# A fused attention and gated-MLP kernel: the planner's prices for VectorE and ScalarE changed, and the order of TensorE's work searched again

## The chip, the cores and the metric

One core of a Trainium2 chip runs the whole program. The metric is the device time of one execution in microseconds (us). The kernel before takes 1592.65 us, the median of three runs (1592.35 to 1593.04).

## What is computed

With x of 2048 tokens by 512 features, 32 query heads of 16 features and one shared key and value head:

```python
q = (x @ wq).reshape(B, S, H, Dh).transpose(0, 2, 1, 3)
k, v = x @ wk, x @ wv
p = softmax(einsum("bhqd,bkd->bhqk", q, k) * Dh ** -0.5)
a = einsum("bhqk,bkd->bhqd", p, v).transpose(0, 2, 1, 3).reshape(B, S, H * Dh) @ wo
b = (sigmoid(x @ w_gate) * (x @ w_up)) @ w_down
g = sigmoid((x * gate_w).sum(-1, keepdims=True))
out = g * a + (1 - g) * b
```

## The kernel before, in words

Everything passes through TensorE and the eight banks of PSUM, each 128 partitions by 512 words of fp32. Attention is cut into 32 units, each of four heads by 512 tokens, and each unit into 16 chunks of 128 keys. A unit needs three kinds of matmul. **Maxima** (function `maximum`, L1126 and L1128): scores with tokens on partitions, of which VectorE takes each row's maximum (TENSOR_REDUCE, 2048 of them in all). **Scores** (`scores`, L1135 and L1137): the same scores with keys on partitions and the maximum already subtracted through an extra row of the contraction, of which ScalarE takes the exponential into a tile p (2048). **Values** (`pv`, L1010): the four p tiles of a chunk against v, as four matmuls side by side in 32 columns each, summed in one bank, which is later copied out into a tile ou (`sums_out`, L1018) by ScalarE or VectorE; where a unit's sum is copied out more than once, GpSimd adds the copies (`sum_add`, L1021). Beside attention stand the **fills** (`fill`, L1105), 4404 matmuls of the MLP and of the output projection, whose results leave their bank in a gate (ScalarE), a product (VectorE) or a scaled copy (`part_of`, L1084 on VectorE or L1086 on ScalarE), or are added onto a tile by VectorE (`add`, L1065). At the start stand the projections of x to keys, values and queries (L864).

Maxima, scores and fills each use 64 rows of the array, so two of them run at once, one in the upper half (h = 0) and one in the lower (h = 1). Such a pair is called a step here. Values use all 128 rows in strips of 32 columns. TensorE goes back and forth between the two shapes: some steps, then a run of values chunks, and so on.

The order of all this is one string, ORDER (L670), found by a search outside the kernel. Each character is a step: a hexadecimal digit packs what the two halves do (0 nothing, 1 a maximum, 2 a score, 3 a fill), `V` is a values chunk, `G` a projection, `T` the turning of a unit's maxima, `C` copies the running sum out so that another bank can take the sums, `.` lets the plan's clock pass 25 units. `plan()` replays the string in a class State, which keeps a clock in its own units and decides by it, while it replays, which bank a matmul takes, which engine makes a copy (`evacuate`), and between which instructions of the other queues loads, stores and GpSimd's tasks go. The instructions are then issued in that order on every engine. At run time nothing of the plan's clock is left: each instruction waits on semaphores for what it needs, and no longer.

State prices work as follows (units of its clock):

```python
self.now += 100                                                   # a step
self.now += VALUES                                                # a chunk of values
if self.full: self.now += OUT                                     # from values to steps
if not self.full: self.now += IN                                  # from steps to values
self.free[i] = self.on("dve", self.now + LATE, RED) + TAIL + FREE # a maximum's bank
at = self.on("act", self.now + LATE_A, EXP) + TAIL_A              # an exponential
self.free[i] = at + FREE_A
```

So a bank read by VectorE counts as free TAIL + FREE units after VectorE's instruction is priced to end, one read by ScalarE TAIL_A + FREE_A units after its own; and a step may only take a bank that the plan has as free. SUM is the price of VectorE's addition, SCALED that of ScalarE's scaled copy (VectorE's is SCALED_D), LATE_V the time from the last values chunk to the copy of its sum.

Of the kernel before, what the change touches and what calls it, by code (L numbers as in the profile page):

```python
# [53 lines left out]
IN, OUT, VALUES, TURN = 52, 94, 371, 20  # L54
# [15 lines left out]
LATE_V = 130  # L70
# [46 lines left out]
class State:  # L117
# [558 lines left out]
    "f6fedf5dVVVVC67b7bbfdb7bedff7fede7e7efbfededfbdef6ff57VVVVV6edef76fbf6efddebf7b7b7b7bfb7afdb7fefededddVVVC6f6def"
    "edb7b7efbdb7f6fdVV999VVC7e7bf6f6fedb7bedbfdfdTVVVC6deeeddfef6f9ff9dbf6fee7b7fbdef9dbff7bb7777V99aV666V699V659VV6"
    "eddbfb7b7ddVVC6b7bfdbd7ddeVVC6deedfbdbbdfbddbfbededfb76fefedbdbfe77777VVV67baV95aV9a5V6TaV696VC6f9bfdbdfd7aVVC9d"
    "eedfeb77b7VVded9bffb79f6fbdefe7b7e7b7ef7ef6f9feb7ffde5dVVC655VVVC6b6ffdedeb7b7fefdefTbfb7bf7b9fededfe7efeb57VV6a"
    "5V999V699V996V65aV65aV999V656VV9deeddbfde7efeeffb7b7bfbfb7b7e7bfbdffdd5dVVVC69edffedeedfe7f77b7efedebffb7bfdbfbd"  # L680
    "f7757VVVVVC9b77bfe7bdbe7fe7f9fe7beddbfeeTffe7bf7fdedd5VVVVC97bfb7edef9f6f9fedfedef6fbd9fb7ef6f9fff5777VVVV6f6fbd"
    "9fbf6b7f9ffed6fef9fb7edef75VVC9e9ff76fff5aVVVVCdadff67bfb7bdbedfedb7ef6f7eb7ef7edbf9ff6f5dVVVaaTVVVC9bdfb7bdbf9f"
    "b77bedfedef9fe7edbbdfedb76fff6dV9a9V696V669V969V666VC699V669VC669V66aV6a5V996V95aV966VCdeTeeff7bf9b7f9f6fed77VVC"
    "9b77bf9fef9dbf7efed7ddVVVV9e9ffdedef9fbdb7ffde7bfeedefde7ff7b7b7777VVVVC97bfbdb7b7efe76fe7fedbf9def6faf7def9fedf"
    "f75VVVC7bTbfef9ff9b7fbd9fedddVVVC6b7fe7b7b7bfe7bffb7be7e7e7fefb67VVVC9f9fedb7bf9ef7e7fe7fdddddVVV9e6f7fede7eeVVV"
# [12 lines left out]
    "ef6bdfbdbdbf7e7bff7775VVVVV6b97ffed7be7bff9fed7fbebff7e7fedeedb7f7ddVVVVC97bfededbb7bf7eeddfbededfe7be7f9fedbfe7"
# [540 lines left out]
```

## Time and profile before

| | |
|---|---|
| median of three runs | 1592.65 us |
| the profiled execution's own time | 1592.79 us |
| its span, first to last instruction | 1591.0 us |
[...]
| VectorE busy | 1406.1 us (88%) |
| ScalarE busy | 1194.6 us (75%) |
| GpSimd busy | 909.2 us (57%) |

The profiled execution lies 0.14 us over the median and 1.8 us over its own span. The busy time of TensorE is that of pipelined matmuls whose ends are modelled, so 99% says that some matmul was always under way, not that none came late. How fast TensorE really goes is read from when its instructions start, in the chain of waits and the timeline.

### The profile page before, as it was taken

The page shows a single profiled execution, that of the slowest core. Times are in us where ns is not written, and L with a number is a line of the kernel's source. Part 1 is how long each engine was busy: PE and PEld are TensorE (multiplying, and loading weights), DVE is VectorE, ACT ScalarE, POOL GpSimd, SP SyncE. Part 2 cuts the span into 40 slices and gives each one's busy share as a digit, 9 for nine tenths or more (in the row PEclk, how much of TensorE's full clock was granted, in tenths as well). Part 3 has the DMA queues.
Part 4 walks back from the last instruction along what each step waited for, and adds up shares of the span by engine and source line. Part 5 has one row for each costly group of instructions (what it writes and reads, how often), then busy time and mean ns, then how long its engine had stood idle before and what let it go on. Part 6 is the DMA issues. An engine that isn't in the chain of part 4 may idle for free.

```text
span 1591.0 us, 33696 instructions
## 1 busy us (share of the span) xinstructions
PE 1582.7 (99%) x12950; PEld 1008.2 (63%) x12950; DVE 1406.1 (88%) x2443; ACT 1194.6 (75%) x2358; POOL 909.2 (57%) x705
## 2 busy tenths in 40 slices
PE   9999999999999999999999999999999999999998
PEld 7776666566665666565664766666566566666644
DVE  6899989999889988999899989999989989899952
ACT  5266778787788777778778776787877877777797
POOL 4348554737664564674673656565766365568332
PEclk9999999999999999999999999999999999999999
DMA  7412111215121211114121121111512021111011
GB/s 229 149 51 71 54 40 38 59 31 137 35 75 31 76 59 45 42 55 104 55 72 32 59 68 42 49 58 32 137 29 81 24 83 59 45 42 31 9 36 44
DMA packets 52230, 98.12 MB, mean 62 GB/s; under 512 B 17960, under 2 KB 19240, under 8 KB 51044
## 3 DMA queue, kind: packets, MB, share of 16 engines
q1 hardware_dynamic: 52068, 95.96, 20.4%
q8 instruction: 101, 1.65, 0.4%
q14 instruction: 61, 0.50, 0.1%
HBM read 74.05 MB, written 8.90 MB: 52 GB/s over the span
## 4 chain that ended last, share of the span: by engine, by line
PE 99%; DVE 0%; DMA 0%; ACT 0%; SPq 0%; issue 0%; DVEq 0%; ACTq 0%
PE bank L1105 32%; PE bank L1010 30%; PE bank L1135 17%; PE bank L1126 16%; PE bank L864 3%; DMA xf<-x_in 0%; DVE mx L1128 0%; PE bank L995 0%; PE bank L1178 0%; ACT x L782 0%; PE bank L934 0%; SPq L767 0%; DVE ba L1187 0%; DVEq L1235 0%; ACT q L956 0%
## 5 line engine op out<-in xcount | busy, mean ns | idle before, releaser
L1128 DVE TENSOR_REDUCE mx<-bank 128x1 f32<-128x512 f32 x2048 | 1258.7, 680 | 121.9 <-PE bank L1126 80.7
L1137 ACT ACTIVATE p<-bank 128x512 f32<-128x512 f32 x2048 | 1038.1, 657 | 46.4 <-PE bank L1135 27.6
L1135 PE MATMUL bank<-qs,ks 64*128 64x512 f32 x2048 | 730.9, 405 | 0.0
L1126 PE MATMUL bank<-ks,qs 62*128 62x512 f32 x2048 | 694.4, 406 | 0.0
L1010 PE MATMUL bank<-p,v_aug 128*32 128x512 f32 x4096 | 487.2, 598 | 0.0
L1135 PEld LDWEIGHTS bank<-qs,ks 64*128 64x128 f32 x2048 | 354.2, 185 | 132.0 <-issue 32.7
L1126 PEld LDWEIGHTS bank<-ks,qs 62*128 62x128 f32 x2048 | 346.4, 185 | 121.8 <-DVE mx L1128 40.9
L1018 ACT COPY ou<-bank 128x512 f32<-128x512 f32 x135 | 79.5, 589 | 291.8 <-PE bank L1010 213.1
L1105 PE MATMUL bank<-wd,hl 64*128 64x512 f32 x1344 | 271.6, 391 | 0.0
L1010 PEld LDWEIGHTS bank<-p,v_aug 128*32 128x32 f32 x4096 | 109.6, 109 | 244.1 <-issue 212.6
L1021 POOL TENSOR_TENSOR ou<-ou,ou 128x512 f32<-128x512 f32 x106 | 137.1, 1293 | 138.1 <-ACT ou L1018 135.1
L1105 PEld LDWEIGHTS bank<-wd,hl 64*128 64x128 f32 x1344 | 201.6, 185 | 15.6
L1105 PE MATMUL bank<-x,wu 64*128 64x512 f32 x672 | 185.8, 392 | 0.0
L1105 PE MATMUL bank<-xs,wg 64*128 64x512 f32 x672 | 185.1, 392 | 0.0
L1105 PE MATMUL bank<-x,wg 64*128 64x512 f32 x672 | 183.9, 391 | 0.0
L1105 PE MATMUL bank<-xs,wu 64*128 64x512 f32 x672 | 182.6, 392 | 0.0
L982 POOL TENSOR_TENSOR qs<-stage,qs 16x1024 fp32r<-16x1024 f32 x62 | 148.6, 2396 | 4.8
L1105 PEld LDWEIGHTS bank<-x,wg 64*128 64x128 f32 x672 | 111.8, 185 | 9.3 <-issue 2.0
L1105 PEld LDWEIGHTS bank<-x,wu 64*128 64x128 f32 x672 | 112.6, 185 | 7.6 <-POOL wg L839 0.8
L1105 PEld LDWEIGHTS bank<-xs,wu 64*128 64x128 f32 x672 | 111.6, 185 | 5.8
L1105 PEld LDWEIGHTS bank<-xs,wg 64*128 64x128 f32 x672 | 111.1, 185 | 6.1
L1089 POOL TENSOR_TENSOR ba<-ba,pa_d 128x512 f32<-128x512 f32 x48 | 61.9, 1289 | 89.9 <-DVE ba L1065 77.6
(92 smaller groups left out, 1129.7 us busy)
## 6 DMA issues: line engine op xcount, KB each, us to landing
rg<-wg SPq DMA_DIRECT2D x28, 512.0 KB
ru<-wu SPq DMA_DIRECT2D x28, 512.0 KB
rd<-wd SPq DMA_DIRECT2D x28, 512.0 KB
stage<-qd SPq DMA_DIRECT2D x192, 64.0 KB
xs<-x SPq DMA_DIRECT2D x16, 512.0 KB
xf<-x_in SPq DMA_DIRECT2D x16, 256.0 KB
qd<-q SPq DMA_DIRECT2D x16, 256.0 KB
ra<-wo SPq DMA_DIRECT2D x8, 512.0 KB
```

Of the source, the lines that this page charges most:

```text
L864: nc.tensor.matmul(ps, w[:, p, part(kc)], X[b, kc][:, q, :], start=i == 0, stop=i == 3 * KC - 1)
L982: e.tensor_tensor(qs[r], stage[r], f32(qs[r]), op=ALU.subtract)
L1010: nc.tensor.matmul(ps[32 * j:32 * j + 32, :], v_aug[:, c, :], PT.pop((u, c, j)), start=new, stop=last)
L1018: (nc.scalar.copy if e == "act" else nc.vector.tensor_copy)(OU[i], ps)
L1021: nc.gpsimd.tensor_tensor(OU[n], OU[n], OU[i], op=ALU.add)
L1089: nc.gpsimd.tensor_tensor(BA[b, t], BA[b, t], PA.pop((b, t)), op=ALU.add)
L1105: nc.tensor.matmul(banks[i], l, r, start=at == 0, stop=at == j.n - 1)
L1126: nc.tensor.matmul(banks[i], qs_t[u % 3][r, pr, part(qt)], ks[r, kb * 512:(kb + 1) * 512], start=True, stop=True)
L1128: nc.vector.tensor_reduce(MX[u][:, pr, h, qt, kb:kb + 1], banks[i], axis=AX.X, op=ALU.max)
L1135: nc.tensor.matmul(banks[i], ks[r, part(c)], qs_t[u % 3][r, pr, :], start=True, stop=True)
L1137: nc.scalar.activation(p, banks[i], AF.Exp, scale=0.25)
```

## The change

Five lines of prices and one string. No function, tile, buffer or instruction kind changes.

```diff
-LATE, LATE_A, FREE, FREE_A = 190, 200, 65, 60
+LATE, LATE_A, FREE, FREE_A = 190, 200, 48, 62
-RED, GATED, SUM, ENDS, PARTS, INVERSE = 260, 258, 285, 60, 325, 70
-EXP, COPY, SCALED = 208, 210, 247
+RED, GATED, SUM, ENDS, PARTS, INVERSE = 257, 258, 288, 60, 325, 70
+EXP, COPY, SCALED = 209, 210, 258
-IN, OUT, VALUES, TURN = 52, 94, 371, 20
+IN, OUT, VALUES, TURN = 52, 94, 369, 20
-LATE_V = 130
+LATE_V = 120
 ORDER = (
-    "GGGGGGGG555G555G555G555GG555GG555GGG555GG555G555G555Gdd55GTfffdf777ff7f777ffffffefb7edbf7b7f9fb7efdef79ffedbe7de"
+    "GGGGGGGG555G555G555G555GGG555G555GG555GGG555G555G555G555GT7ffff7fdffdf7fff7f77fee7ef76fef7ffde7ef97bbfdbdf9fbbdd"
...
```

The rest of ORDER is another string of the same kind. Counted in the two strings, and in the instructions that come of them:

| | before | after |
|---|---|---|
| values chunks | 512 | 512 |
| runs of values chunks (of one chunk; of five) | 230 (93; 11) | 222 (88; 21) |
| runs of projections | 12 | 12 |
| steps (with one half empty) | 4256 (12) | 4257 (14) |
| `.` | 2 | 10 |
| `C` | 106 | 101 |
| copies of a sum, L1018: ScalarE; VectorE | 135; 2 | 129; 3 |
| scaled copies: ScalarE, L1086; VectorE, L1084 | 59; 21 | 49; 31 |
| GpSimd's additions of sums, L1021 | 106 | 101 |

Every other kind of instruction keeps its count on every engine, and so do the transfers on SP's queue.

On TensorE, in unit 3, before: chunks 10 and 11 of the values (the second number in the name of p) stand alone between three steps each.

```order
L1010 MATMUL bank2_74<-p3_10_0_0_3301,v_aug_105 32x512
L1010 MATMUL bank2_74<-p3_10_0_1_3196,v_aug_105 32x512
L1010 MATMUL bank2_74<-p3_10_1_0_3292,v_aug_105 32x512
L1010 MATMUL bank2_74<-p3_10_1_1_3178,v_aug_105 32x512
L1135 MATMUL bank5_77<-qs0_132,ks_128 128x512
L1126 MATMUL bank1_73<-ks_128,qs2_134 128x512
L1135 MATMUL bank6_78<-qs0_132,ks_128 128x512
L1126 MATMUL bank0_72<-ks_128,qs2_134 128x512
L1135 MATMUL bank7_79<-qs0_132,ks_128 128x512
L1135 MATMUL bank3_75<-qs1_133,ks_128 128x512
L1010 MATMUL bank2_74<-p3_11_0_0_3333,v_aug_105 32x512
L1010 MATMUL bank2_74<-p3_11_0_1_3258,v_aug_105 32x512
```
The same unit on TensorE in the change: chunks 9, 10 and 11 follow each other.

```order
L1126 MATMUL bank4_76<-ks_128,qs2_134 128x512
L1010 MATMUL bank3_75<-p3_9_0_0_3119,v_aug_105 32x512
L1010 MATMUL bank3_75<-p3_9_0_1_3230,v_aug_105 32x512
L1010 MATMUL bank3_75<-p3_9_1_0_3101,v_aug_105 32x512
L1010 MATMUL bank3_75<-p3_9_1_1_3191,v_aug_105 32x512
L1010 MATMUL bank3_75<-p3_10_0_0_3156,v_aug_105 32x512
L1010 MATMUL bank3_75<-p3_10_0_1_3238,v_aug_105 32x512
L1010 MATMUL bank3_75<-p3_10_1_0_3126,v_aug_105 32x512
L1010 MATMUL bank3_75<-p3_10_1_1_3234,v_aug_105 32x512
L1010 MATMUL bank3_75<-p3_11_0_0_3197,v_aug_105 32x512
```
What moved: the steps that stood between the chunks now stand before and after the run (unit 3 goes from nine runs of values to six, other units go from fewer to more).

On VectorE, in unit 19's maxima before: the second token tile of block 2 (ba2_1) gets its first part from ScalarE, and VectorE only adds onto it.

```order
L1128 TENSOR_REDUCE mx19_11198<-bank2_74 128x1
L1128 TENSOR_REDUCE mx19_11198<-bank3_75 128x1
L1128 TENSOR_REDUCE mx19_11198<-bank0_72 128x1
L1065 SCALAR_TENSOR_TENSOR ba2_1_11730<-bank1_73,gom_131,ba2_1_11730 128x512
L1128 TENSOR_REDUCE mx19_11198<-bank4_76 128x1
L1128 TENSOR_REDUCE mx19_11198<-bank2_74 128x1
L1128 TENSOR_REDUCE mx19_11198<-bank6_78 128x1
```
The same place on VectorE in the change (the name before the arrow is the tile written):

```order
L1128 TENSOR_REDUCE mx19_11269<-bank5_77 128x1
L1128 TENSOR_REDUCE mx19_11269<-bank4_76 128x1
L1084 TENSOR_SCALAR ba2_1_11676<-bank6_78,gom_131 128x512
L1128 TENSOR_REDUCE mx19_11269<-bank7_79 128x1
L1128 TENSOR_REDUCE mx19_11269<-bank4_76 128x1
L1128 TENSOR_REDUCE mx19_11269<-bank5_77 128x1
L1128 TENSOR_REDUCE mx19_11269<-bank3_75 128x1
L1065 SCALAR_TENSOR_TENSOR ba2_1_11676<-bank0_72,gom_131,ba2_1_11676 128x512
```
What moved: the scaled copy into ba2_1 is now VectorE's, between two maxima, where the maxima behind it come one instruction later.

## Rows read from the trace of the kernel before

**Rows 1.** The page: span, busy time by engine, chain that ended last.

```profile
span 1591.0 us, 33696 instructions
PE 1582.7 (99%) x12950; PEld 1008.2 (63%) x12950; DVE 1406.1 (88%) x2443; ACT 1194.6 (75%) x2358; POOL 909.2 (57%) x705
...
PE 99%; DVE 0%; DMA 0%; ACT 0%; SPq 0%; issue 0%; DVEq 0%; ACTq 0%
PE bank L1105 32%; PE bank L1010 30%; PE bank L1135 17%; PE bank L1126 16%; PE bank L864 3%; DMA xf<-x_in 0%; DVE mx L1128 0%; PE bank L995 0%; PE bank L1178 0%; ACT x L782 0%; PE bank L934 0%; SPq L767 0%; DVE ba L1187 0%; DVEq L1235 0%; ACT q L956 0%
```
**Rows 2.** The two longest waits of TensorE's matmuls, whole span (us, times, longest).

```profile
PE bank L886 <- POOL v_aug L880: 1.3, 1, 1.3
PE bank L1164 <- ACT ou_last L1162: 0.5, 1, 0.5
```
**Rows 3.** The chain in time (start us, us, what), values runs around 210 us.

```profile
205.94 4.43 PE bank L1010 x40
210.37 0.43 PE bank L1126
...
220.64 3.57 PE bank L1010 x32
```
**Rows 4.** Groups of TensorE's matmuls between those two runs, 210.3 to 220.55 us.

```profile
L1105 PE MATMUL bank<-xs,wg 64*128 64x512 f32 x24 | 7.1, 396 | 0.0
L1135 PE MATMUL bank<-qs,ks 64*128 64x512 f32 x19 | 7.0, 395 | 0.0
L1105 PE MATMUL bank<-x,wg 64*128 64x512 f32 x24 | 6.9, 392 | 0.0
L1126 PE MATMUL bank<-ks,qs 62*128 62x512 f32 x19 | 6.6, 400 | 0.0
```
**Rows 5.** The chain in time, values runs of one chunk, 471 to 488 us.

```profile
471.06 0.99 PE bank L1010 x8
...
472.94 1.00 PE bank L1010 x8
...
488.10 1.00 PE bank L1010 x8
```
**Rows 6.** Timeline of VectorE and ScalarE (start us, us) near 401 and 211 us.

```profile
401.12 5.47 DVE L1128 TENSOR_REDUCE mx<-bank 128x1 f32<-128x512 f32 x9 [1.74 <-PE bank L1126]
401.18 5.02 ACT L1137 ACTIVATE p<-bank 128x512 f32<-128x512 f32 x10
...
210.83 11.64 DVE L1128 TENSOR_REDUCE mx<-bank 128x1 f32<-128x512 f32 x19 [1.71 <-PE bank L1126]
```
**Rows 7.** Who waited for the maxima on VectorE, whole span (us, times).

```profile
  PEld bank L1126: 40.9, 51
  PEld bank L1135: 32.2, 39
  PEld bank L1010: 11.6, 35
  PEld bank L995: 3.5, 6
```
**Rows 8.** Groups on VectorE, ScalarE and GpSimd, whole span (count, busy us, mean ns, idle).

```profile
L1128 DVE TENSOR_REDUCE mx<-bank 128x1 f32<-128x512 f32 x2048 | 1258.7, 680 | 121.9 <-PE bank L1126 80.7 <-PE bank L1135 33.4 <-PE bank L1105 4.2
L1084 DVE TENSOR_SCALAR pa_d<-bank,gom 128x512 f32<-128x512 f32 x13 | 9.6, 741 | 0.0
L1018 ACT COPY ou<-bank 128x512 f32<-128x512 f32 x135 | 79.5, 589 | 291.8 <-PE bank L1010 213.1 <-issue 37.4 <-POOL ba L1089 8.2
L1086 ACT ACTIVATE pa_d<-bank,gom 128x512 f32<-128x512 f32 x35 | 25.9, 741 | 0.0
L1021 POOL TENSOR_TENSOR ou<-ou,ou 128x512 f32<-128x512 f32 x106 | 137.1, 1293 | 138.1 <-ACT ou L1018 135.1 <-DVE ou L1018 2.4
```
**Rows 9.** The chain by line in shares of the span, and its longest VectorE piece.

```profile
by line: PE bank L1105 32.5%; PE bank L1010 29.6%; PE bank L1135 16.7%; PE bank L1126 16.1%; PE bank L864 3.3%; DMA xf<-x_in 0.3%; DVE mx L1128 0.2%; PE bank L995 0.2%; PE bank L1178 0.1%; ACT x L782 0.1%; PE bank L934 0.1%; issue 0.1%; SPq
...
61.30 3.59 DVE mx L1128 x6
```

More of the change, by code (lines that the diff above doesn't have):

```diff
@@ L676 @@
[L676 to L685, printed above, removed]
@@ new lines @@
+    "efe7bd9ffedbdb7fddf5VVVVVC99ffb7bdbf9f6fede7fbdee77eefdedbf9fdff77577VVVVC67bb7b7fbb7edfe7f6fedeeddefedbfTefb7fe"
+    "d77f5VVVVC6edeeddeefdbdf9fb7fbdbf97bfb7f6ee7fdff77775VVV9edeededddddVVC9ed7bfb7bbdbdf9ff6fb7bb7b7fbd6f77dVVVC6ef"
+    "76fbe7f6e7fb7ffdd5dVVVC67bfb7bfTbfb7fde7b7fb7bbf7ed7fd5VVVC9deeedddbfbedfeffededeb7defaf5f7VVVVV676fef6feb7e7f6f"
+    "defedbe7f9ef79fbf9dbfbdff7ddddddVVVVC66ffb76f6fef6fb7b7f6fbbdbdfb7bdbf9feddVVVVVCTb7bfbf7b7bb77bbf7bdebdedfedede"
+    "f7eedffdddd5VVVC9eddeeedf7bf9fbdeffedef6ed7efd7dVVVV67b7bb7bb7b77.VVC9b7bfd9fbb77bfe7e7fe7ededbbfdef9fededfd77f5"
@@ new lines @@
+    "VVVVC6b7bb7ffTbfb7ff7e7b7be7e7fe7e7bdVVVC9deeedddeeddd.VVVC67b7b7b7b7bbff9ff9fedef67eef76feedf9fedf7fe7f577VVV96"
+    "9V6bdbfdbdb7ddVVCdedee5dVVC6e7fb7edeedfb7bb77fb7be7fededebbdfdbf7edef9VV65TVVC6b7bfdbdedbdVVVC97bbb7ffb7eb7f9ffb"
+    "f9fef67bfe7e7eedfe7f6fedef7fddddd5VVV6a5V9a5V995VVC6defe7bdbdef6f6fbdfbdebdbdf6fbdebd7efbbf777VV9a6V6a6V9a6V6aTV"
+    "65aVC999V6a5VVVC67bb77efedbf6f6fbffb79fbb7b7fbd7VVV9dedeeddbfbdbfbdfefe7e7eefdfdd5dVVVC9edefdb7ef9bf7efdf7757VVV"
+    "C9dbbf79fb7bfb76ffbdeeddbfe7edeedfTfefe7f776VVVVVC6b77bbb7ff97bfbdf9fb7e7ededefe7eedf6ffbfe7b777ddVVVVV9f9bdfb7e"
@@ new lines @@
+    "f97bfbdf6f6fededef6f6fffdddd5VVVVC6e77efedebdfed6ffedbf9dbfbdbdb7b7bfef6f7b7eVV6T9V55aVVVC6dedeedfe7ef9fe7defb7b"
+    "b7b7bfdbdb7e7bfbdfbddV9a5Va66V6a5V669V696V699V999V6a5V6a5V9a5V6a5VC6a5V9a5V9aTV699VC6b7b7bb77fbbffb7fb76fbede7ef"
+    "7fd5VVVC6dedeededeefffeddefb7bf6bf7fdd5dVVV69dfbfbdbdee7fdeff7775VVVC6eddedefef97bfb7b7f9fbb77eefdef9b7fbdeffd7T"
+    "VVVVVC76fe7edefe7bdeb7bdffdfbfbb7f6f9fb7ffdd5ddVVVVC67bb77bfe7ee7fedeffb7bf6bfbf7afdfdfddddddVVVV67bfb79fbf9f9fe"
+    "7e7fbd9fedbef79fedee7f6fffd6VVVVVC9defededee7bdfbdbdfbd6fef6fb7bfTefb7bffadf7d7dVVVVVC99bff7e7bf9f6ff6f9fedb7bde"
@@ new lines @@
+    "fede7ef7f77757VVVC9debf79fafdedf7efeb777VVV9dadff6f9fef6f6f7bfd7bVVVC6dedeef7afde7fbd7bfe7eedb7f9fbfbdbTfeffbb75"
+    "VVVVVC67b7bbb7f7bfbe7fe7fbd9fbe7effb67VVC9ededeedddddd.VVVC67b7bbb7b7fef7e7e7fe7bf9e7fedef9dbf7dbfbfde77dddVV9a5"
+    "V9e7fe7e7e7e7VVC9deddddVVVC6b7fededeefTfbf9fbf9b77fb7edef6feb77bfafddeVVC9e6f7f9fbd7dVV666VC9dbefdb7bdebVa66V959"
+    "VV659VV6dedeefdb7eedfe7e7fbdebdf6f6fb7bb7b7fbdff75VVC969V959VVVCdedafdf6f6fe7eb7b7fedef9f7ef9b7fbdedbb7fbdb4VV6a"
+    "9V6aTV666V966VC999V969V669V95aV669V996VC9debfdbdbdb7efedfdfedededeffbff7b7b777777VVVVC67a7ffe76feb7fbdfbfe7efbbf"
@@ new lines @@
+    "Tfbf6fbfede5ddddVVVVVC6ededdeeeedf7fbddefbd6fb7bb7fbdb7bb7ff9fdffd5dddVVVVV67bdef6fef6f6f6fbdfe7b7bf9bf79fbf7f7d"
+    "5VVVVC9edeed7fef6b7fb7defeedb7bfdedbf9ffTbfb7f77aVVVVVC97b7b7bfbdbdbfedf9fb7edb7edbf6feededfe7eff9Va65V6a6VVVVV9"
+    "dbbfdbdbdbbdfbdf6fbdeedb7bfdedbe7f9f6fdf77VV666V696VC6a5V6a5V699VC9deededdeeffTfffb6ff9defed6fdf75VVVC67b7bbb7bf"
+    "7fbfb7dbfe7be7efdfd577VVVC9ededdbfbedbdfbdf77777VVV6b7fbdb7afdedfb7b7fed6fbdbefdedef6edff777d7VVVVC6eddefeeTffb7"
+    "bf79bffb5VVVC9adffd6fafdedffef9fbdef9edfefe6eVVVVC67b7bbb7bfdf9ffbfb7b7b7efe7e7f6eVVVVV6b7b77bfbb7f9f9fdbf9fedeb"
@@ L716 @@
+    "bb7bffb7bbf7b77bf9fe7bef7e7e7e7efe7edffdeddd5dVVVVVCd6fededefbdbde7eef7be7f6bf7b7fedbfTbfb7f7d5VVVVC9deefd9fedeb"
+    "dfefbdfbdbdebdef7eeeVVVC6b77b7b7bbbb7.V655VVV9deeddbfbdedefaffdfbdb7bfefb7bb7f9fbdbfdb25.Va66V666V9a6Va6aVVa96V9"
+    "aaVVC66aVaaTVVabbaVVCbfbbfbfeeeeee8VVeeeeeeeeVVebffbfbfbfeeeeVbbaaVVbbaaVVbbaaVVbbaaVVabffbfbfffbeeeVVaeeecccccc"
+    "88cccVVV"
 )
```

49 lines of the change are left out of this document (15 added, 34 removed).

## The prediction

> **What bounds the kernel now.** I read the page first. It gives TensorE 99% of the span and gives it 99% of the chain that ended last; VectorE, at 88%, holds next to nothing of that chain [rows 1]. The second view is the waits of TensorE's own matmuls: the longest in the whole span are 1.3 us at the very start and 0.5 us in the closing stage [rows 2]. So the end is set by how fast TensorE goes through its order, and what has to be priced is the kinds of step in that order. Third, the chain in time shows this price. A run of five values chunks takes 4.43 us and one of four 3.57 us [rows 3], so a chunk is worth 4.43 - 3.57 = 0.86 us, and 4.43 - 5 x 0.86 = 0.13 us is left over for entering and leaving the run. Between these two runs lie 220.64 - 210.37 = 10.27 us of steps. The groups of that stretch have 24 + 19 + 24 + 19 = 86 matmuls, which is 43 steps of two [rows 4].
>
> The short rounds give the rest. From 471.06 to 488.10 us stand nine rounds of one chunk and three steps each (so the order string has them), 17.04 / 9 = 1.893 us a round [rows 5]. A chunk alone takes 0.99 us, which leaves 0.90 us for three steps with their entry. Against the long stretch, a step is (10.27 - 0.90) / 40 = 0.234 us. A round therefore holds 0.86 us for its chunk, 3 x 0.234 = 0.70 us for its steps, and 1.893 - 0.86 - 0.70 = **0.33 us for going from one shape of matmul to the other and back**. TensorE does nothing useful in this 0.33 us, and it falls due once a round, whatever the round holds.
>
> **The change part by part.** *Rounds.* The change has the same 512 chunks in 222 runs in place of 230, and as many runs of projections. Eight times the pair of switches goes: 8 x 0.33 = 2.6 us, all of it on the path, as TensorE is the path. *Steps.* 4257 in place of 4256, as two more have an empty half: + 0.23 us. *VALUES from 371 to 369, IN, OUT and TURN as they were.* A planner's clock is not the chip's: the chunk takes 0.86 us at either price, so this edit by itself is worth nothing. The work that could turn up in its place is none, since no instruction changes.
>
> *Copies of sums.* Five fewer closes of a bank: ScalarE makes six fewer copies at 0.59 us, VectorE one more, GpSimd five fewer additions at 1.29 us [rows 8]. This lies beside TensorE. ScalarE is idle for a quarter of the span and GpSimd for 43% [rows 1]; what it costs is nothing, and what it gives is nothing either, unless one of them had been late for TensorE, which rows 2 don't show. *Scaled copies.* Ten move from ScalarE (0.74 us each) to VectorE (0.74 us each) [rows 8]. With the one copy of a sum VectorE gets 11 x 0.74 = 8.1 us more. It sat idle for 121.9 us ahead of its maxima, waiting for TensorE [rows 8]; that idle time is the cover. If it were gone at the places where the copies stand, each of the copies would push the maxima behind it, and the banks they hold, back by up to 0.74 us, 8.1 us in all.
>
> *The margins.* A bank read by VectorE was taken as free 260 + 38 + 65 = 363 units after its maximum could start, and is now so after 257 + 38 + 48 = 343. A step is 100 units and 0.234 us, so a unit is 2.34 ns and the cut is 20 units or 47 ns. Is 257 right? In the densest stretch near 401 us nine maxima take 5.47 us; with 0.68 us for the last, as the group's mean has it [rows 8], the pace is (5.47 - 0.68) / 8 = 0.599 us [rows 6], or 256 units. In the stretch at 211 us nineteen take 11.64 us, a pace of 0.609 us or 260 units [rows 6]. I take 0.599, because the longer stretch may hold pauses in which VectorE waited for TensorE and a dense one cannot beat the engine. By 0.609 the plan is 4 units or 9 ns short for each maximum, 0.17 us over a stretch of nineteen; the margin behind the end, 38 + 48 units or 0.20 us, still covers that. So I cost the margins at 0, with bounds from both sides. Above: the trace has 51 + 39 + 35 + 6 = 131 places where TensorE's weight loads waited until a maximum was done [rows 7]; if each comes late by the whole cut, that is 131 x 47 ns = 6.2 us. Below: VectorE's maxima hold 0.2% of the chain, 3.2 us, of which 3.59 us as one piece stand at 61 us in the first stage [rows 9] (shares are rounded); if a better fit of the order takes half of that off, 1.6 us.
>
> The exponentials go the other way: nine and a bit of them, 0.66 us for the last, make a pace of about (5.02 - 0.66) / 9 = 0.484 us or 207 units [rows 6]. The old 208 and the new 209 both cover it, and the new one has two units more of margin. Worth 0.
>
> [...]
>
> **The sum.** 1592.8 (the profiled execution, 0.14 us over the median of the runs) - 2.6 + 0.2 = **1590.4 us**. Something near 0.2%, 3.2 us, is what a measurement of this kernel can tell from no change; faster means under 1589.5 us, slower over 1595.8 us. The forecast is a small gain that stays inside that.
>
> **The rivals.**
>
> *The switches were not all lost time (gain swallowed).* Longer runs of values need the exponentials of more chunks to be there at once, and longer stretches of steps put more maxima and exponentials in a row, so the eight pairs of switches saved could come back as short waits for ScalarE or VectorE in front of runs. For it: the change has 21 runs of five where there were 11, and ten pauses planned in place of two. Eight more pauses of 25 units would be 8 x 25 x 2.34 ns = 0.5 us if TensorE really had to wait in each. Against: ScalarE is busy for 75% only. All the gain gone: 1592.8 us.
>
> *Waits go as well (faster).* The new prices lie nearer to the pace of rows 6, so the small waits that make up VectorE's 0.2% of the chain [rows 9] could shrink by the half priced above: 1590.4 - 1.6 = 1588.8 us. For it: the first stage has TensorE following VectorE closely at 61 us. Against: the waits that the trace names for matmuls are so small already that little can be taken off [rows 2].
>
> *VectorE comes late (slower).* The same cut that lets the plan take a bank 47 ns earlier makes TensorE stand at a bank that VectorE still reads; since TensorE's queue is in order, all behind it stands too. Place: the first steps after runs of values and the long stretches of steps, where the maxima of rows 7 are waited for, above all where a scaled copy now sits between two maxima. Price: 6.2 us, so 1590.4 + 6.2 = 1596.6 us. It decides from the point where these 131 places lose more than (1595.8 - 1590.4) / 131 = 41 ns each on the average, nearly all of the cut. Against it: VectorE idles for 121.9 us, and 0.2 us of margin remains behind each of its instructions.
>
> *The pace is wrong from the start (slower).* If a maximum could only start when the one before it has ended, 0.68 us by the group's mean [rows 8], the old price of 260 units (608 ns) would be wrong nearly as much as the new one, and only the difference of 3 units would be new: 2048 x 3 x 2.34 ns = 14.4 us if every one of them bound, 1590.4 + 14.4 = 1604.8 us. Rows 6 exclude it, but for a stretch read wrongly. [...]
>
> *Nothing happens (no effect).* Were the order on TensorE held by something that the string doesn't move, the time would stay at 1592.8 us. Only the closing stage and the start are like that, and they are the same in both; I count this with the swallowed gain.
>
> **How the numbers follow.** Forecast (1589.5 to 1592) 0.57; gain swallowed or nothing happens 0.16; waits go as well 0.20; VectorE late 0.06; pace wrong 0.01. The rival of fewer waits ends at 1588.8 us, so it carries the chance of faster: 0.20. The forecast and the swallowed gain are within 0.2%: 0.73. The other two make slower: 0.07. The range for 8 in 10 reaches down to the faster rival with 0.3 us for the rounding of 0.33 us (8 x 0.04), 1588.5 us, and up past the swallowed gain by the 0.5 us of the pauses, 1593.3 us.
>
> **What would show it.** In the profile after, runs of one chunk should still repeat every 1.89 us with three steps, a run of five take 4.43 us, and TensorE's matmul waits stay at about 2 us in all; then the 2.4 us are the rounds. Right for the margins: who waited for the maxima stays near 131 times with the same 0.8 us at most. Wrong: a row of TensorE waiting for a maximum or a scaled copy by name, steps that take clearly over 0.234 us in a stretch of some forty, or VectorE's maxima at a pace over 0.609 us without a pause. The prediction fails on the rounds if the time per round is the same and the end is not 2 to 3 us earlier.

## The result, and the profile after

| us | before | after |
|---|---|---|
| median of 20 runs each | 1592.72 (1592.11 to 1593.21) | 1594.67 (1594.03 to 1597.0) |
| span of the profiled execution | 1591.0 | 1592.4 |

The change is slower by 1.95 us: the ratio is 1.0013, its interval 1.0007 to 1.0019. That is inside the 0.2% which the prediction counts as no change, but on the other side of the old time, 4.3 us from the forecast of 1590.4 us and 1.4 us over the top of its range.

The page of the kernel after, the lines that answer to [rows 1]: span, busy time, the chain that ended last by engine.

```profile
span 1592.4 us, 33640 instructions
...
PE 1583.6 (99%) x12950; PEld 1009.3 (63%) x12950; DVE 1408.8 (88%) x2454; ACT 1184.5 (74%) x2342; POOL 902.2 (57%) x700
...
PE 97%; ACT 2%; DVE 1%; POOL 0%; issue 0%; DVEq 0%; ACTq 0%; POOLq 0%
```

TensorE has lost two points of the chain, and ScalarE and VectorE have them. Where, the chain in time says (start us, us, what); the first lines answer to [rows 3, 5, 9].

```profile
61.19 3.60 DVE mx L1128 x6
...
112.36 6.88 ACT p L1137 x14
...
122.09 3.57 PE bank L1010 x32
...
208.82 4.43 PE bank L1010 x40
...
473.43 0.99 PE bank L1010 x8
475.31 1.00 PE bank L1010 x8
...
490.46 0.99 PE bank L1010 x8
...
1099.48 6.88 ACT p L1137 x14
...
1199.10 2.50 DVE mx L1128 x4
```

The prices of a round are what they were. A run of five takes 4.43 us, one of four 3.57 us, and nine short rounds of three steps take (490.46 - 473.43) / 9 = 1.892 us each, against 1.893 before. So the eight rounds were saved: 8 x 0.33 = 2.6 us less, and one step of 0.23 us more. New are the pieces at 112, 1099 and 1199 us, and shorter ones at 257 and from 581 to 587 us, of which the chain before has none. Each of them leads up to one of the turns described below.

To find what took the gain back I measured every stretch of steps between two runs of values: from its first matmul to the first of the next run, less 0.205 us and 0.2325 us for each step. (These two constants give 0.90 us for three steps, as [rows 5] have them, and 10.20 us for 43, where [rows 3] have 10.27.) What is over counts as waiting; the sums hang on the two constants, their difference hardly, as both kernels have the same steps but one. Summed over all stretches it is 5.35 us before and 9.36 us after: **4.0 us of new waits**, 2.9 in the 32 stretches that hold a turn `T`, 1.2 in the others. The account closes: - 2.6 + 0.2 + 4.0 = + 1.6 us, with 1.4 us between the spans.

*The turns.* A unit's maxima end in a finishing reduction on VectorE, which writes the tile mm (L987), and TensorE's transposes of mm (L995) are the turn. The view of mm, what the engines sat idle for before these instructions (us, times), in the kernel before:

```profile
  DVE mx L1128: 2.5, 3
  issue: 1.7, 2
  DVE mm L987: 1.0, 3
  ACT p L1137: 0.9, 2
```

and after:

```profile
  ACT p L1137: 3.6, 8
  issue: 2.0, 3
  DVE mm L987: 1.1, 3
  DVE mx L1128: 0.8, 1
```

The timeline after, around the turn of the second unit:

```profile
112.17 6.67 DVE L1128 TENSOR_REDUCE mx<-bank 128x1 f32<-128x512 f32 x11 [1.14 <-PE bank L1135]
...
118.68 0.39 PE L1105 MATMUL bank<-x,wu 64*128 64x512 f32 x1
118.88 0.22 DVE L987 TENSOR_REDUCE mm<-mx 128x16 f32<-128x64 f32 x1
119.01 0.68 DVE L1128 TENSOR_REDUCE mx<-bank 128x1 f32<-128x512 f32 x1
...
119.21 0.12 PEld L995 LDWEIGHTS bank<-consts,mm 64*16 64x16 f32 x2 [0.58 <-ACT p L1137]
119.24 0.23 PE L995 MATMUL bank<-consts,mm 64*16 64x64 f32 x2 [0.17 <-ACT p L1137]
```

The profile puts the wait down to ScalarE's exponential. It is VectorE: its finishing reduction ends at 118.88 + 0.22 = 119.10 us, and the transposes start 0.14 us later, while the two banks they write had been free for 0.99 and 0.51 us. In seven turns of the change the transposes start 0.145 us after that reduction, in three more 0.054 or 0.055 us: ten turns of 32 are bound by VectorE, where four were before. In the ten, the gap from the matmul before the transposes is 0.25 to 0.56 us, against 0.23 us in a turn that waits for nothing, 2.0 us over in all (0.4 us in the four before). The plan lets a turn start at the very unit at which its VectorE has finished (the line `self.maxima.append((u, self.on("dve", 0, ENDS)))`), with no margin at all. It also has that moment too early. The finishing reduction starts 0.71 to 0.73 us after the last maximum started, in 62 of the 64 turns of the two kernels, not 0.60 us as a further maximum would, and takes 0.22 us: its end lies 0.34 us, 144 units, behind the place at which a further maximum could start, where ENDS says 60. It also holds VectorE for longer, as the next instruction starts another 0.137 us later as a rule (here 119.01 - 118.88 us): 108 units in place of 60.

*The banks.* The timeline after, behind one of VectorE's scaled copies:

```profile
642.08 0.75 DVE L1084 TENSOR_SCALAR pa_d<-bank,gom 128x512 f32<-128x512 f32 x1 [0.17 <-issue]
...
642.74 1.88 DVE L1128 TENSOR_REDUCE mx<-bank 128x1 f32<-128x512 f32 x3
...
643.31 0.39 PE L1135 MATMUL bank<-qs,ks 64*128 64x512 f32 x1
643.48 0.18 PEld L1126 LDWEIGHTS bank<-ks,qs 62*128 62x128 f32 x1 [0.21 <-DVE mx L1128]
643.48 0.50 PE L1126 MATMUL bank<-ks,qs 62*128 62x512 f32 x1
```

The first of the three maxima ends at about 642.74 + 0.68 = 643.42 us, and the matmul that takes its bank starts at once behind it, 0.17 us after its partner in the other half. Before, three matmuls in the whole span (a projection at 65 us aside, which does so in both kernels) took a bank less than 0.12 us after the end of the maximum that read it; after, 39 do, eleven of them within 0.06 us. (Behind ScalarE's exponentials, whose prices EXP and FREE_A went up, there are 13 such takes where there were 29.) The 39 are not spread evenly: 12 come in a stretch without a pause behind a scaled copy on VectorE and 12 others behind a finishing reduction, 31% each, though only 8% and 10% of all maxima stand so. The three before all come behind a finishing reduction. The view of who waited for the maxima, which answers to [rows 7]:

```profile
  PEld bank L1135: 40.2, 64
  PEld bank L1126: 37.1, 50
  PEld bank L1010: 15.7, 47
...
  PEld bank L995: 1.9, 4
```

64 + 50 + 47 + 4 = 165 weight loads of these four lines wait where 131 did. And VectorE's groups, which answer to [rows 8]:

```profile
L1128 DVE TENSOR_REDUCE mx<-bank 128x1 f32<-128x512 f32 x2048 | 1257.0, 683 | 118.8 <-PE bank L1126 75.4 <-PE bank L1135 41.1 <-PE bank L995 0.2
...
L1084 DVE TENSOR_SCALAR pa_d<-bank,gom 128x512 f32<-128x512 f32 x21 | 15.6, 744 | 0.2 <-issue 0.2
```

Nothing there is slower: 683 ns where 680 stood, 118.8 us of idle time where 121.9 did. The 4.0 us do not show in any sum by engine.

### The profile page after: what moved, and what is told of

The parts are those of the page before. It is cut to its first block, busy times and chain, and to the rows that moved or that the text cites. A ratio compares the mean times of both kernels' runs of the same rounds, so it can differ in the third digit from the quotient of the medians.

```text
span 1592.4 us, 33640 instructions
## 1 busy us (share of the span) xinstructions
PE 1583.6 (99%) x12950; PEld 1009.3 (63%) x12950; DVE 1408.8 (88%) x2454; ACT 1184.5 (74%) x2342; POOL 902.2 (57%) x700
## 4 chain that ended last, share of the span: by engine, by line
PE 97%; ACT 2%; DVE 1%; POOL 0%; issue 0%; DVEq 0%; ACTq 0%; POOLq 0%
PE bank L1105 33%; PE bank L1010 29%; PE bank L1135 15%; PE bank L1126 15%; PE bank L864 3%; ACT p L1137 1%; DVE mx L1128 0%; PE bank L886 0%; PE bank L995 0%; ACT ou L1018 0%; POOL wd L758 0%; PE bank L1178 0%; PE bank L934 0%; POOL ou L1021 0%; POOL wd L757 0%
## 5 line engine op out<-in xcount | busy, mean ns | idle before, releaser
L1128 DVE TENSOR_REDUCE mx<-bank 128x1 f32<-128x512 f32 x2048 | 1257.0, 683 | 118.8 <-PE bank L1126 75.4
L1137 ACT ACTIVATE p<-bank 128x512 f32<-128x512 f32 x2048 | 1033.5, 654 | 42.9 <-PE bank L1135 19.4
L1135 PE MATMUL bank<-qs,ks 64*128 64x512 f32 x2048 | 720.3, 406 | 0.0
L1018 ACT COPY ou<-bank 128x512 f32<-128x512 f32 x129 | 75.8, 588 | 304.4 <-PE bank L1010 220.9
L1105 PE MATMUL bank<-wd,hl 64*128 64x512 f32 x1344 | 279.7, 392 | 0.0
L1021 POOL TENSOR_TENSOR ou<-ou,ou 128x512 f32<-128x512 f32 x101 | 130.5, 1292 | 113.1 <-ACT ou L1018 108.8
L757 POOL CAST hl<-h 128x512 fp32r<-128x512 f32 x56 | 34.2, 611 | 131.7 <-DVE h L1115 131.4
```

The lines of the kernel that those rows point to most:

```text
L757: hi(hl[:, 0, :], raw)
L1018: (nc.scalar.copy if e == "act" else nc.vector.tensor_copy)(OU[i], ps)
L1021: nc.gpsimd.tensor_tensor(OU[n], OU[n], OU[i], op=ALU.add)
L1105: nc.tensor.matmul(banks[i], l, r, start=at == 0, stop=at == j.n - 1)
L1128: nc.vector.tensor_reduce(MX[u][:, pr, h, qt, kb:kb + 1], banks[i], axis=AX.X, op=ALU.max)
L1135: nc.tensor.matmul(banks[i], ks[r, part(c)], qs_t[u % 3][r, pr, :], start=True, stop=True)
```

## The experiments

Fifteen kernels ran. "Us" is the median, with that of the kernel before on the same chip; "waits" is the sum over the stretches of steps as above; "turns" and "banks" are the turns that start within 0.17 us of VectorE's finishing reduction, and the banks taken within 0.12 us of a maximum's end.

| kernel | us (before) | ratio, interval | waits | turns | banks |
|---|---|---|---|---|---|
| before | 1592.72 | 1 | 5.35 | 4 | 3 |
| the change | 1594.67 (1592.72) | 1.0013, 1.0007 to 1.0019 | 9.36 | 10 | 39 |
| e1 turns later | 1593.33 (1592.64) | 1.0005, 0.9996 to 1.0014 | 8.45 | 2 | 39 |
| e2 448 columns | 1590.45 (1592.64) | 0.9987, 0.9978 to 0.9996 | 5.34 | 9 | 1 |
| e3 448 columns, old kernel | 1592.46 (1592.64) | 0.9999, 0.999 to 1.0007 | 4.98 | 3 | 0 |
| e4 old order, all new prices | 1594.27 (1592.64) | 1.001, 1.0002 to 1.0019 | 6.69 | 4 | 11 |
| e5 old order, FREE 48 | 1593.41 (1592.87) | 1.0004, 0.9995 to 1.0013 | 5.94 | 4 | 4 |
| e6 old order, FREE 100 | 1594.45 (1592.87) | 1.001, 1.0001 to 1.0019 | 7.01 | 4 | 6 |
| e7 turns later, FREE 65 | 1594.24 (1592.87) | 1.001, 1.0 to 1.0019 | 9.51 | 2 | 39 |
| e8 turns later, FREE 100 | 1594.94 (1592.87) | 1.0015, 1.0006 to 1.0023 | 9.92 | 2 | 37 |
| e9 504 columns | 1592.50 (1592.82) | 0.9998, 0.9989 to 1.0007 | 7.19 | 10 | 11 |
| e10 488 columns | 1591.51 (1592.82) | 0.999, 0.9982 to 0.9999 | 6.57 | 10 | 2 |
| e11 scaled copies on ScalarE | 1605.32 (1592.82) | 1.0076, 1.0063 to 1.0089 | 18.92 | 10 | 24 |
| e12 turns later, 504 columns | 1591.21 (1592.94) | 0.9993, 0.9984 to 1.0002 | 6.62 | 2 | 15 |
| e13 change's order, safer prices | 1592.31 (1592.94) | 0.9995, 0.9986 to 1.0003 | 7.04 | 9 | 7 |
| e14 old order, safer prices | 1592.44 (1592.94) | 0.9997, 0.9988 to 1.0005 | 5.10 | 3 | 5 |
| e15 e13, turns later | 1591.77 (1592.51) | 0.9995, 0.9986 to 1.0004 | 7.48 | 2 | 13 |

The waits account for the times: - 2.4 us for rounds and step plus the waits over 5.35 gives + 0.7 for e1 (measured + 0.69), - 2.4 for e2 (- 2.19), - 0.6 for e9 (- 0.32), - 1.2 for e10 (- 1.31), - 1.1 for e12 (- 1.73), - 0.7 for e13 (- 0.63) and - 0.3 for e15 (- 0.74): good to some 0.3 us, but for 0.6 us in e12 and 0.5 us in e15.

In the quoted expectations A is the turn, D the margin behind VectorE's reads, P the price of a maximum and S the scaled copies that moved to VectorE; B, E and F are their rivals, by which the loss sits elsewhere.

### Is it VectorE at all? (e1, e2, e3)

e1 is the change with eight of its turns two steps later (and without the assert that a bank is free by the plan's clock, so that the rest of the plan can stay); one of the lines of ORDER:

```diff
-    "efe7bd9ffedbdb7fddf5VVVVVC99ffb7bdbf9f6fede7fbdee77eefdedbf9fdff77577VVVVC67bb7b7fbb7edfe7f6fedeeddefedbfTefb7fe"
+    "efe7bd9ffedbdb7fddf5VVVVVC99ffb7bdbf9f6fede7fbdee77eefdedbf9fdff77577VVVVC67bb7b7fbb7edfe7f6fedeeddefedbfefTb7fe"
```

> The change with eight of its 32 turns of maxima (T) put two steps later in ORDER: the eight whose transposes start 0.145 us or less after VectorE's last reduction of the unit in the trace of the change and that follow a step. Theory A (the turn comes too early for VectorE: the plan lets a turn start at the very moment its clock has VectorE's last reduction done, and the old 260 units had hidden that): the eight gaps of 0.40 to 0.56 us in front of the turns fall to about 0.23 us, 1.8 us in all, and the time to 1592.5 to 1593.2 us. Rival B (TensorE waits for banks that are read late by VectorE or ScalarE, whatever stands in front): the gaps move to the steps around the turn, and the time stays within 0.6 us of the change, 1594.1 to 1595.3 us.

e2 is the change with maxima over 448 of the 512 columns (the last 64 columns of each block of keys are left out of the maximum), which shortens VectorE's work (a maximum takes 617 ns in place of 683, by the means of the groups) and leaves TensorE's and ScalarE's alone; e3 is the same cut on the kernel before.

```diff
-        nc.vector.tensor_reduce(MX[u][:, pr, h, qt, kb:kb + 1], banks[i], axis=AX.X, op=ALU.max)
+        nc.vector.tensor_reduce(MX[u][:, pr, h, qt, kb:kb + 1], banks[i][:, :448], axis=AX.X, op=ALU.max)
```

> [...] Theory A and B alike, as far as VectorE is the late one (A the turn, B the banks): the 4.0 us that the steps take over their own 0.2325 us go back to 2 us or less, time 1591 us or less. Rival C (ScalarE is the late one: its exponentials hold 1.3% of the chain after and nothing before): time within 1 us of the change, 1593.7 to 1595.7 us.

> The kernel before with each maximum over 448 of 512 columns, the same cut as in the run on the change (the last 64 columns are left out of the maximum). If VectorE's lateness is what the change pays for its fewer rounds, the kernel before gains little here (1591 to 1592.3 us), and with VectorE out of the way the change beats it by the price of its eight rounds and one step, 2.0 to 2.8 us. By rival C the two stay 2 us apart the other way.

e2 is decisive: 1590.45 us, faster than the kernel before by 2.2 us, with its waits back at 5.34 us. The same cut gave the old kernel 0.2 us. (The intervals of e2 and e3 just touch, but the spans of their eleven runs each lie apart: 1587.7 to 1588.5 us and 1589.6 to 1591.1.) So with VectorE out of the way the change is worth 2.0 us, the rounds nearly in full, and what took it back hangs on how long a maximum lasts. VectorE's group in e2 and the chain by engine on its page:

```profile
L1128 DVE TENSOR_REDUCE mx<-bank 128x1 f32<-128x448 f32 x2048 | 1158.7, 617 | 203.2 <-PE bank L1126 114.6 <-PE bank L1135 66.8 <-PE bank L1105 2.2
```

```profile
PE 99%; DVE 0%; ACT 0%; DVEq 0%; issue 0%; POOL 0%; POOLq 0%
```

e1 takes off 1.26 us against the change, each set against its own kernel before (its interval and the change's overlap; the trace is plainer). The view of the tile mm and the page's chain of e1:

```profile
  issue: 2.0, 3
  DVE mx L1128: 0.8, 1
  DVE mm L987: 0.6, 2
```

```profile
PE 99%; DVE 0%; ACT 0%; issue 0%; DVEq 0%; POOL 0%; ACTq 0%; POOLq 0%
```

The eight waits that the profile put down to ScalarE are gone, and so are the pieces of ScalarE in the chain at 112 and 1099 us, though ScalarE has the same work to do: moving the turn away from VectorE's reduction did that. 8.45 us of waits remain, so the turns are a part of it, not all. The eight gaps held 1.9 us over the 0.23 us of a free turn and the waits fell by 0.9: with its turns moved, e1 takes a bank at 41 places before its own plan has it free, so part of what it gains at the turns may be lost again at banks.

### Which edit? The old order under new prices (e4 to e8)

e4 replays the old ORDER with all the change's prices, e5 with `FREE, FREE_A = 48, 62` alone, e6 with FREE at 100; e7 and e8 are e1 with FREE at 65 and 100. Like e1 they go on where a bank is not yet free by the plan's clock: this happens 43 times in e4, 10 in e5, 195 in e6, 117 in e7 and 240 in e8.

```diff
-LATE, LATE_A, FREE, FREE_A = 190, 200, 65, 60
+LATE, LATE_A, FREE, FREE_A = 190, 200, 48, 62
```

> The old ORDER replayed with the new prices: TensorE's order is that of before, only a few scaled copies change engine (VectorE 23 to 24 in place of 21 of the 80) and some tasks of the other queues move. If the time of the change comes from the searched string, this is the kernel before within 0.5 us (1592.2 to 1593.2 us). If it comes from where the prices put copies and tasks, it is slower by 1 us or more.

> The kernel before with FREE and FREE_A at 48 and 62, all other prices and ORDER as before: each step does the same work, no copy changes engine, and 130 of the 4574 takes of a bank get a bank that another instruction had held. Theory D (the prices set which of the free banks a step takes, and a smaller margin behind VectorE than behind ScalarE sends steps to banks that VectorE still reads): slower than before by 0.4 us or more, 1593.0 to 1594.3 us. Rival E (which bank is taken makes no difference; the 1.6 us of the old order with all new prices came with the three copies and the moved tasks): within 0.3 us of before, 1592.3 to 1592.9 us.

> The kernel before with FREE at 100 in place of 65, the plan's check of the bank left out: the same order, 745 of 4574 takes get another bank, as steps now keep off VectorE's banks and go to ScalarE's. D: if the 65 was about right, ScalarE's exponentials become what is waited for, 1592.8 to 1594 us; were VectorE's banks still the late ones, under 1592.3 us. E: 1592.3 to 1592.9 us.

> The change with its eight turns two steps later (as run before, 1593.33 us) and the banks chosen with FREE at 65. D: 0.4 to 1 us less than with 48, 1592.3 to 1592.9 us. E: 1593.0 to 1593.6 us.

> The same with FREE at 100. D: VectorE ends its maxima later against the plan than ScalarE its exponentials only by what the traces show, so this should keep steps off VectorE's late banks and bring most of the 2.9 us that the narrow maxima took off: 1591 to 1592.5 us, or, if ScalarE becomes the late one, over 1593 us. E: 1593.0 to 1593.6 us.

Measured: e4 1594.27 us (+ 1.63), e5 1593.41 (+ 0.54), e6 1594.45 (+ 1.58); e7 1594.24 and e8 1594.94, both with higher medians than e1's 1593.33 (e7's interval overlaps with e1's). This line of attack failed, and it fails for a reason worth keeping. The wider margin of e6 cost more than the narrower one of e5, since an order that is replayed under prices other than those it was searched with gets other banks (some 370 of the 4574 takes of a bank differ in e4, 130 in e5, 745 in e6), picked by a clock that no longer fits the order. With the wider margin the late takes move to ScalarE: those within 0.12 us of an exponential's end go from 29 in the kernel before to 61 in e6, and from 18 in e1 to 44 in e8. So e4 to e8 don't separate the cut of FREE from a misfit, and the theory that a wider FREE on the change's order would help fell with e7 and e8. They do speak against the choice among the free banks as what makes the 39 late takes: the old order has 4 with FREE at 48, and the change's order keeps 39 with FREE at 65. What each price is worth in an order searched with it stays open.

### Which part: the price of a maximum, the copies, the turn (e9 to e12)

e9 and e10 leave 8 and 24 columns out of each maximum of the change, in the same way as e2. By the means of the groups, 683 ns in the change and 617 ns in e2, a column is 66 / 64 = 1.03 ns, so 8 columns are 8 ns or 3.5 units of 2.34 ns: about what the price 260 had over 257, and a fifth of the 17 units, 40 ns, by which FREE was cut. 24 columns are 25 ns by this, and two maxima give more than those 40 ns back; the mean in e10 is 657 ns, 26 ns less than in the change. (From start to start, where VectorE has no pause, e9's maxima follow each other after 590 ns, the median, and the change's after 598.)

```diff
-        nc.vector.tensor_reduce(MX[u][:, pr, h, qt, kb:kb + 1], banks[i], axis=AX.X, op=ALU.max)
+        nc.vector.tensor_reduce(MX[u][:, pr, h, qt, kb:kb + 1], banks[i][:, :504], axis=AX.X, op=ALU.max)
```

> [...] Theory P (it is the price of a maximum: 3 units each add up over a stretch and come late together, at the turn above all): more than half of the 4.2 us that 64 columns brought, 1591.5 to 1592.5 us. Theory F (it is the margin FREE, 17 units or 0.040 us once for each bank): 8 columns bring a fifth or less, 1593.8 to 1594.6 us.

> [...] P: what 8 columns left is nearly gone, 1590.6 to 1591.5 us. F: between, 1591.8 to 1593.5 us, as a stretch of only two maxima already gives the 0.040 us back.

e9 came out at 1592.50 us: 8 ns a maximum bring back 2.2 of the 4.2 us that 64 ns bring (0.3 us under its own kernel before, against 1.95 over). The banks taken in the last moment fall from 39 to 11. The ten turns stay bound, as nine do in e2: what they wait for is the finishing reduction and the 0.145 us behind it, which shorter maxima leave as they are. e10 takes another 1.0 us. Both came out at the upper end of what theory P expects, but they don't exclude F: in a stretch of five maxima 8 ns each are 40 ns, the whole cut of FREE, and many stretches are longer than that. So e9 gives the size of VectorE's lateness, a few units a maximum, and not which of the two lower prices let it show.

e11 issues all 31 scaled copies that the change gives VectorE on ScalarE instead; the plan still counts them on VectorE.

```diff
-        if e == "dve":
+        if False:
```

> The change with all scaled copies issued on ScalarE, the plan and with it every bank, every step and every place of the others as in the change: 31 copies leave VectorE (about 0.66 us of its time each) and come to ScalarE. Theory S (VectorE is late because of the ten more scaled copies, which the plan prices at 264 units): 1 us or more faster than the change, 1592.5 to 1593.7 us. P and F: no gain, and ScalarE, which the plan does not know to have them, is late in their place: 1594.5 to 1597 us.

1605.32 us, 12.5 over the kernel before, and waits of 18.9 us. The expectation fell, whichever way the copies were meant to count. The page's busy time of e11, its chain, and pieces of that in time:

```profile
PE 1592.8 (99%) x12950; PEld 1006.2 (63%) x12950; DVE 1392.7 (87%) x2423; ACT 1202.3 (75%) x2373; POOL 902.3 (56%) x700
...
PE 94%; ACT 4%; POOL 1%; DVE 1%; DMA 0%; issue 0%; SPq 0%; DVEq 0%; ACTq 0%; POOLq 0%
```

```profile
1521.63 4.42 ACT p L1137 x9
...
1551.34 3.89 ACT p L1137 x8
1556.46 4.50 ACT p L1137 x10
1561.08 3.22 ACT p L1137 x6
1564.87 3.92 ACT p L1137 x8
```

31 copies of 0.75 us that the plan doesn't know of cost (1605.32 - 1594.67) / 31 = 0.34 us each, on an engine that is busy for 75% of the span. The idle quarter of ScalarE covered here only about half of the copies' time, 0.34 us of each 0.75 being lost, in an order that was searched to the unit.

e12 has both cures, e1's turns and e9's 504 columns.

> Both cures at once: the eight turns two steps later (alone: 1593.3 us) and maxima over 504 of 512 columns (alone: 1592.5 us; the maximum leaves out the last 8 columns). One lateness (the turns are only the place where the shortfall of 3 units a maximum shows): the second cure finds little left at the turns and the two don't add, 1592.0 to 1592.6 us. Two separate costs (a turn has no margin of its own, a maximum is priced too low): the gains of 1.3 and 2.2 us add, 1590.8 to 1591.6 us.

1591.21 us: against the change, e1 took off 1.26 and e9 2.27 us (each set against its own kernel before), together 3.5; e12 takes off 3.7. The medians add, so turn and price look like two separate costs. The waits add less well, 0.9 and 2.2 us apart and 2.7 together, and the intervals of e9 and e12 overlap, so this is as far as the runs carry it. The chain of e12, in which no piece of ScalarE's exponentials or VectorE's maxima of a microsecond is left:

```profile
PE 99%; ACT 0%; DVE 0%; issue 0%; DVEq 0%; POOL 0%; ACTq 0%; POOLq 0%
```

### A version with safer prices (e13, e14, e15)

e13 is the change's order, improved by many small exchanges (two steps, a half of a step, a turn) that were accepted where a plan with safer prices ended sooner: the old prices of a maximum and of the margin, VectorE's scaled copy at 283 units, a turn 62 units after its maxima. Nothing of the computation is left out. The plan waits where the kernels before and after assert. The prices of the edit and the turn's line stand below; the string and the lines by which the plan waits are left out. e14 is the same from the old order, and e15 is e13 with seven turns two steps later still.

```diff
-LATE, LATE_A, FREE, FREE_A = 190, 200, 48, 62
+LATE, LATE_A, FREE, FREE_A = 190, 200, 65, 62
-RED, GATED, SUM, ENDS, PARTS, INVERSE = 257, 258, 288, 60, 325, 70
-EXP, COPY, SCALED = 209, 210, 258
+RED, GATED, SUM, ENDS, PARTS, INVERSE = 260, 258, 285, 60, 325, 70
+EXP, COPY, SCALED = 209, 210, 250
-COPY_D, SCALED_D = 262, 264
-LATE_V = 120
+COPY_D, SCALED_D = 262, 283
+LATE_V = 125
-            self.maxima.append((u, self.on("dve", 0, ENDS)))
+            self.maxima.append((u, self.on("dve", 0, ENDS) + 62))
```

> The change's order with small exchanges searched under safer prices (maximum 260, margins 65 and 62, scaled copy on VectorE 283, a turn ready 62 units after its maxima are finished, the rest as in the two kernels); still 222 runs of values and 4257 steps. By its plan it ends 616 units or 1.4 us before the kernel before replayed under the same prices. If the loss is VectorE's prices and the turn's missing margin, that gain shows: 1590.6 to 1592.0 us, faster than both. If the loss hangs on something these prices don't count (longer runs of values that want more exponentials at once), it stays near the change: 1593.3 to 1595.0 us.

> The order of the kernel before with small exchanges searched under the same safer prices; 229 runs of values and 4256 steps. By its plan it ends 304 units or 0.7 us before the kernel before under the same prices. If safer prices by themselves take out waits: 1591.7 to 1592.4 us. If the kernel before has nothing to win there, as the cut of 64 columns on it found (0.2 us): 1592.4 to 1593.0 us.

> The climbed order of the change (1592.3 us) with seven of its turns two steps later: in its trace nine of 32 turns still start 0.06 or 0.15 us after VectorE's last maximum of the unit is finished, so 62 units were too little, and the gaps at these seven are 0.75 us longer in all than the 0.23 us of a turn that waits for nothing. Turn and price are separate costs (as the two cures that added up say): 1591.0 to 1591.7 us, about 1.3 to 1.9 us faster than the kernel before. If the turns are not what is left: 1592.1 to 1592.6 us.

e13 takes 1592.31 us: 2.6 us better than the change against their own kernels before, with intervals that don't meet (0.9986 to 1.0003; 1.0007 to 1.0019), and 0.6 us under the kernel before, which its interval doesn't tell from nothing. (The spans point the same way more clearly: 1588.6 to 1590.1 us in its eleven runs, 1590.0 to 1591.6 in the 27 of the kernel before.) It missed the 1590.6 to 1592.0 that were expected. e14, the control, is at 1592.44 us. In e13 the banks taken late are down to 7, but nine turns are still bound: 62 units are the 0.145 us from reduction to transposes and leave nothing for the finishing reduction, whose end ENDS has 84 units too early. e15 moved seven of them and missed too. It stands 0.74 us under its kernel before, where 1.3 to 1.9 had been expected and e13 had 0.63; bound turns fell to two, the banks taken late rose to 13 and the waits to 7.48 us. So e13 and e15 have the lowest medians of the kernels that leave nothing out, but no run shows them faster than the kernel before beyond the interval, and about 2 us of waits over the kernel before are left in both. Which price makes those, the runs don't settle. ENDS, which none of them changed, is the first to try: three of e13's seven late takes and seven of e15's 13 come behind a finishing reduction.

## Why the prediction was wrong

*The rounds* were right: eight fewer, 1.892 us a short round, 4.43 us a run of five, and 2.0 of the 2.4 us seen in the time itself once VectorE was out of the way (e2 against e3).

*The margins* were the step that failed: "the margin behind the end, 38 + 48 units or 0.20 us, still covers that. So I cost the margins at 0". The bound above, 6.2 us, was stated and then put aside; the measured new waits are 4.0 us, of which some 1.6 us stand at the turns, where the bound had six of its 131 places. Three things were wrong in the argument. First, the margin was not 0.20 us. A maximum's own record ends 0.683 - 0.599 = 0.084 us, 36 units, behind the place at which the next one starts, so TAIL, 38 units, is no margin but the end of the maximum itself. Of the other 50 units the handoff to TensorE takes at the least 0.053 us, 23 units. What is left is 27 units or 0.06 us, where the kernel before had 44. And I compared the pace with the price: 256 units against 257, so 257 covers it. The pace was right, and the eleven maxima that end at 118.84 us in the change show it again: (6.67 - 0.68) / 10 = 0.599 us. But 260 against 256 had not been a mistake that the change put right: the four units to spare in each maximum made good what the plan has too short elsewhere. An estimate from these rows: behind a finishing reduction, which holds VectorE for 108 units and is priced at 60, VectorE is 48 units late, which a dozen maxima make good at a price of 260, and three to four times as many at 257. e9 gives back 8 ns a maximum and with it 2.2 us. How the loss is shared between the 3 units of RED and the 17 of FREE, no run shows.

Second, one thing the plan underprices grew with the change. The timeline after, VectorE around 700 us:

```profile
691.38 4.28 DVE L1128 TENSOR_REDUCE mx<-bank 128x1 f32<-128x512 f32 x7 [0.41 <-PE bank L1126]
695.57 0.74 DVE L1065 SCALAR_TENSOR_TENSOR ba<-bank,gom,ba 128x512 f32<-128x512 f32 x1
696.23 4.96 DVE L1128 TENSOR_REDUCE mx<-bank 128x1 f32<-128x512 f32 x8
701.11 0.74 DVE L1084 TENSOR_SCALAR pa_d<-bank,gom 128x512 f32<-128x512 f32 x1
701.76 0.74 DVE L1065 SCALAR_TENSOR_TENSOR ba<-bank,gom,ba 128x512 f32<-128x512 f32 x1
702.42 1.28 DVE L1128 TENSOR_REDUCE mx<-bank 128x1 f32<-128x512 f32 x2
```

A scaled copy holds VectorE for 701.76 - 701.11 = 0.65 us, or 278 units (281 by the median of the change's 24 that are followed without a pause, 0.658 us), where SCALED_D says 264: 14 to 17 units short, 31 times in place of 21. I counted such copies at nothing under 121.9 us of idle time. Of the 39 late takes 12 come behind one. What of the 4 us is theirs, no run shows: e11, which was to tell, put the load on an engine that could not take it.

Third, I looked for the margin in banks alone. A turn waits for VectorE with no margin at all, a unit's last stretch of maxima ends in one, and ENDS prices the reduction between them too low, which is no part of the change: the new order only puts more turns close behind it. Ten bound turns against four: 1.26 us by e1.

*The cover* was wrong as a kind of argument: "It sat idle for 121.9 us ahead of its maxima, waiting for TensorE [rows 8]; that idle time is the cover." The idle time was there after as well (118.8 us), and TensorE waited all the same: it stands before the runs of maxima, and the handoffs are at their ends. e11 shows it from the other side, with 75% of ScalarE busy and 0.34 us lost for each copy.

*The rivals.* "VectorE comes late" was the right mechanism at the right places, banks behind maxima and behind a scaled copy, and it had a chance of 0.06. That TensorE keeps its order, so that what stands behind a late bank waits too, both traces show: of their 12950 matmuls only neighbours, at most three, start in another order than the program's. Its price needs no new row: 131 x 47 ns at full, and by the measured waits 4.0 / 131 = 31 ns each, or 19 ns at the other 125 places without the turns' 1.6 us, under the 41 ns from which I let it decide. I had made it all or nothing; halfway, it swallows the gain and 1.95 us more. "Gain swallowed" stopped at 1592.8 us as if what eats a gain ended at its size. And of what would show it wrong, the longest waits by name stayed useless: in the list of what TensorE's matmuls waited for, only 0.2 us of the new 4.0 us is to be seen, as "PE bank L995 <- ACT p L1137: 0.2, 1, 0.2", which blames ScalarE. Waits of 0.05 to 0.3 us vanish there.

*Small terms.* One step more and fewer copies of sums gave no sign of their own. The exponential at 209 with FREE_A at 62 may have: the late takes behind exponentials fell from 29 to 13, but no run tried these prices in an order searched with them alone (e5, with FREE_A at 62 on the old order, has 28). LATE_V at 120 and VALUES at 369 were not tried alone.

## What to carry to other kernels

In a plan that is packed to the unit, a price above the measured pace is a margin that grows along a run of equal instructions. Before it is cut to the pace, look for what is priced too low or not at all (a handoff between engines, a dependent step at the run's end) and give that its price; and before something is called a margin, take off it the record's own end. Idle time of an engine over the span was no cover for it here (118.8 us of it, and 39 banks taken late): count how often the consumer starts directly behind the producer's end, before and after. And a bound that can't be excluded belongs in the range, at a part of its size too.

## What the runs showed of the hardware

A transpose started at the least 0.054 us after the VectorE instruction that it waits for, and in seven turns of the change 0.145 us after it, within a nanosecond of each other; matmuls started at the least 0.053 us after the end of the maximum whose bank they take. A maximum of 512 columns follows the one before it after 0.599 us though its own record is 0.68 us long, but a scaled copy or a scaled addition holds VectorE for 0.65 to 0.66 us, and a reduction of the maxima themselves starts only 0.035 us behind the end of the last one's record. And 8 columns of a maximum, 8 ns of the 598 from start to start, moved a program of 1.6 ms by 2.2 us, more than 0.1%.
